# A two-layer linear-attention and Mish kernel: another order of work in its first block

## The chip, the cores and the metric

The kernel runs on one core of a Trainium2 chip. The metric is the device time of one execution in microseconds (us). The median of the three runs of the kernel before is 1381.55 us (1381.36 to 1382.13).

## What is computed

Two equal layers act on x of 2048 rows by 640 columns, in fp32. Each layer adds a linear attention of the normalized rows, and then a dense block of the normalized rows:

```python
q, k, v = split(layernorm(x) @ wqkv)              # 32 heads of 20
pq, pk  = q @ w_phi[h], k @ w_phi[h]              # per head, 20 x 20
phi     = concat(softmax(p), softmax(-p))         # 40 features for a head, of pq and of pk
kv, z   = phi_k^T v, sum of phi_k over the rows
x = x + ((phi_q kv) / (phi_q z + 1e-6)) @ wo
x = x + mish(layernorm(x) @ w1 + b1) @ w2         # 640 -> 1536 -> 640
```

Both layers use the same weights.

## The kernel before

**Tiling.** The rows are worked in 8 blocks of 256, each block as two tiles of 128 rows. Columns go in 5 chunks of 128 (KD = 5) where they are contracted. Every operand of a large product is split into a high part in the fp32r format (an ACT copy) and a low part that is the rest (a subtraction), and a product is three matmuls: high by high, high by low, low by high. One projection of one row tile (`project`, L329, its matmuls L344) is thus 2 column halves by 5 chunks by 3 = 30 matmuls of 128 x 320.

**Stages of a layer.** `attend_first` (L387) goes over the blocks. For each row tile it makes keys k, values v and queries q. `features` (L355) turns a k or q projection into softmax features, with ACT, VectorE (DVE) and GpSimd (POOL: the subtraction L369 of queries, the multiplication L379). Keys and values are summed over all rows into one PSUM tile `kva` (L416), and the query features are written to DRAM. `attend_second` (L549) reads them back, applies kv and the output weights wo, and prepares the weights of the dense block; `dense` (L677) does the rest. In the second layer the folded query and key weights come back from DRAM, where the first layer put them (`spill_qk_weights`, L187).

**Folding.** The matrix w_phi of a head is multiplied into the query and key columns of wqkv once, in the first layer. The host lays w_phi out as `phi_bd`, 120 x 6 x 120: block-diagonal groups of 6 heads (120 rows), and a sixth group of 2 heads (40 rows). `load_raw` (L212) fetches the transposed weights (`wqk_t`) in five tiles of 120 rows and one of 40; `fold_phi` (L227) multiplies chunk by chunk. For each of the 5 chunks there are two halves: columns 0 to 360 (tiles 0 to 2) and 360 to 640 (tiles 3 to 5), each with three matmul calls (L237), then the ACT copy L242 and the VectorE subtraction L243 that split the result. A call of plain fp32 is two matmul instructions in the trace, so a fold is 60 instructions.

**The first block of the first layer** (L446 to L460) is the place of the change. SP issues the DMAs. `tc.manual_schedule(engines={SP})` makes SP's issues keep the order written: half of phi, three raw tiles of the query weights, x of block 0, the other half of phi, the other raw tiles. `fetch_normed(0)` (L389) takes the row statistics (`norm_stats`, L246, on VectorE; `norm_scale`, L255, on POOL and VectorE). `normed(0, xt).all()` scales the two row tiles on ACT and turns them: `Transposed.step` (L271) turns 2 chunks of both row tiles on TensorE (four transposes by the identity, L280; two in the last step), and splits the result (ACT L285 through `act`, VectorE L286). Then come the query fold, values' weights (`load_v_weights`, L167, each chunk through `split`, L123, into a staging tile), and the raw key weights.

**The loop over blocks** (L465) follows. In block 0 the order is v0, q0, v1, k0, q1, k1, with the key fold ahead of k0 (L480). While block b is worked, x of block b + 1 is fetched and its statistics taken (at n = 0), scaled (n = 2) and turned (n > 2). Behind block 1, `load_o_weights` (L205) runs `make_five` (L193) to its end: five fetches of wo, five ACT copies (L148) and five POOL subtractions (L149).

**What sets the order of instructions.** The whole stands in a block that the framework schedules by a simulated timeline (L812): each engine's instructions go out in the order that the scheduler finds, except on engines named in a `manual_schedule`, which keep the order written. `act` (L110) chains ACT's instructions that go through it; `tc.issue_after(ins)` puts an engine's following instructions behind `ins`. A tile of a pool takes a buffer that is free: 4 row tiles (tag xn), 2 v tiles, 5 big tiles, and in PSUM 4 tiles of one bank (`one_tile`) and 2 of two banks (`mm_tile`).

Of the kernel before, what the change touches and what calls it, by code (L numbers as in the profile page):

```python
# [16 lines left out]
P = 128  # L17
# [24 lines left out]
def kernel(  # L42
# [42 lines left out]
    make_identity(nc, ident)  # L85
    b1s = const.tile([P, KF], F32, name="b1s")
# [21 lines left out]
    last_act = [None]  # L108

    def act(*args, **kw):  # L110

        if last_act[0] is None:
            ins = nc.scalar.activation(*args, **kw)
        else:
            with tc.issue_after(last_act[0]):
                ins = nc.scalar.activation(*args, **kw)
# [6 lines left out]
    def split(hi, lo, src, stage):  # L123

        st = stage()[:, :D]
        nc.sync.dma_start(st, src)
# [39 lines left out]

    def load_v_weights():  # L167

        ws = [r1_pair(k) for k in range(KD)]
        for k in range(KD):  # L170
            split(ws[k][0][:, D:2 * D], ws[k][1][:, D:2 * D], wv[k * P:(k + 1) * P, :],
                  (row_tile, row_tile, v_tile, v_tile, big_tile)[k])
# [32 lines left out]
    def load_o_weights():  # L205
        return list(make_five(KD, lambda k: wo[k * P:(k + 1) * P, :]))[1:]

# [4 lines left out]
    def load_raw(which, ts=range(6)):  # L212

        raw = []
        for t in ts:
            rows = 120 if t < 5 else 40
# [6 lines left out]
            nc.sync.dma_start(r[:n], wqk_t[which * D + t * 120:which * D + t * 120 + n, :])  # L223
# [3 lines left out]
    def fold_phi(ws, bd, raw):  # L227

        pss = {}
        for k, c in ((0, 0), (1, 0), (2, 0), (3, 0), (0, 1), (1, 1), (2, 1), (3, 1), (4, 0), (4, 1)):  # L230
# [3 lines left out]
            ps = pss[k][c]  # L234
            for t in range(3 * c, 3 * c + 3):
                r, rows = raw[t]
                nc.tensor.matmul(ps[:, (t % 3) * 120:(t % 3) * 120 + rows],  # L237
                                 r[:rows, k * P:(k + 1) * P], bd[:rows, t, :rows],
                                 start=True, stop=True)
# [147 lines left out]
    def attend_first(layer, x_src, first):  # L387


        def fetch_normed(b):  # L390
            if layer:
                return load_turned(n2_d[b], [row_tile] * 3)
            xt = fetch(x_src, b)
# [38 lines left out]
        def values(xts, i, v):  # L432
            vv = v.rearrange("p (h d) -> p h d", d=DH + 1)
            act(vv[:, :, DH], ident[:, :H], AF.Copy, scale=0.0, bias=1.0)
            if i < BT:
                pv = project(xts, i, kv_ws, D, [one_tile(), one_tile()])
# [9 lines left out]
        if first is None:  # L446
            with tc.manual_schedule(engines={mybir.EngineType.SP}):
                bd = big_tile()[:120, :720].rearrange("p (t c) -> p t c", t=6)
                nc.sync.dma_start(bd[:, :3], phi_bd[:, :3])
# [445 lines left out]
```

## Time and profile before

| | |
|---|---|
| Median of the runs | 1381.55 us |
| Profiled execution, its own time | 1381.04 us |
| Its span, first to last instruction | 1379.0 us |
| Mean granted TensorE clock | 0.999 |
| TensorE (PE) busy | 1364.3 us, 99% of the span |
| VectorE (DVE) busy | 1077.0 us, 78% |
| ScalarE (ACT) busy | 583.3 us, 42% |
| GpSimd (POOL) busy | 441.0 us, 32% |

How to read the profile: times count from the span's start. A row of the timeline has the start, the length, the engine, the line of the kernel, the operation, out<-in by the program's names, the shapes, and how many instructions are merged in it; in brackets stands the idle time before it and what ended it. Matmuls overlap in the pipeline and their ends are modelled, so the distance between starts says more than a length. PEld is the loading of stationary operands. A row of the window view has the stretch, its length, each engine's busy time with its instructions, TensorE's granted clock, the DMA engines' share and GB/s. A row of DMA issues has out<-in, the issuing queue, the count, KB of one and the median us from issue to landing.

### The profile page before, as it was taken

How to read it: one execution, taken by the hardware profiler on the slowest of the kernel's cores; microseconds unless marked ns; L12 is line 12 of the kernel's file. 1: busy time of each engine (PE TensorE's matmuls, PEld its weight loads, DVE VectorE, ACT ScalarE, POOL GpSimd, SP SyncE). 2: the span in 40 equal slices, each digit the busy share in tenths (PEclk: the TensorE clock that was granted, in tenths of full speed). 3: DMA queues.
4: the chain of work that ended last, by engine and by line, in shares of the span. 5: the costliest groups of instructions: out<-in, count | busy, mean ns of one | idle time of the engine just before them, and what ended most of it. 6: DMA issues, size and time to landing. Idle time of an engine off the chain costs nothing.

```text
span 1379.0 us, 30804 instructions
## 1 busy us (share of the span) xinstructions
PE 1364.3 (99%) x12866; PEld 1350.7 (98%) x12866; DVE 1077.0 (78%) x1820; ACT 583.3 (42%) x971; POOL 441.0 (32%) x334
## 2 busy tenths in 40 slices
PE   7999999999999999999999999999999999999998
PEld 7999999999999999999999999999999999999998
DVE  5799977886698887788769898988668776677775
ACT  4444434222355444545454333432235444354443
POOL 1353543353322221222234434453342111111112
PEclk9999999999999999999999999999999999999999
DMA  8532433779624533344473433458965321333200
GB/s 321 173 67 62 73 54 61 211 227 316 227 68 96 115 90 62 80 116 96 117 262 74 95 59 59 70 117 274 297 239 163 77 53 45 97 96 96 77 20 19
DMA packets 350277, 169.67 MB, mean 123 GB/s; under 512 B 287098, under 2 KB 323690, under 8 KB 350138
## 3 DMA queue, kind: packets, MB, share of 16 engines
q1 hardware_dynamic: 350137, 167.72, 45.0%
q8 instruction: 100, 1.64, 0.5%
q14 instruction: 40, 0.32, 0.1%
HBM read 104.76 MB, written 62.91 MB: 122 GB/s over the span
## 4 chain that ended last, share of the span: by engine, by line
PE 94%; DVE 2%; DMA 1%; issue 1%; POOL 0%; SPq 0%; ACT 0%; DVEq 0%; POOLq 0%; ACTq 0%
PE mm L344 26%; PE one L691 24%; PE mm L733 24%; PE one L344 12%; PE mm L569 3%; PE one L280 2%; PE one L416 2%; PE mm L237 1%; DMA raw<-in_wqk_t 1%; DVE m L368 1%; PE one L237 0%; DMA v<-in_wv 0%; DVE big L371 0%; DVE r L377 0%; DMA raw<-in_wo 0%
## 5 line engine op out<-in xcount | busy, mean ns | idle before, releaser
L733 PE MATMUL mm<-r2h,ol 128*128 128x320 f32 x1280 | 305.0, 309 | 0.3 <-ACT ol L716 0.3
L717 POOL TENSOR_TENSOR ol<-big,ol 128x512 fp32r<-128x512 f32 (+1 forms) x98 | 130.4, 1330 | 483.6 <-ACT ol L716 407.4
L691 PE MATMUL one<-xtl,r1h 128*128 128x256 f32 x960 | 268.2, 279 | 0.0
L691 PE MATMUL one<-xth,r1l 128*128 128x256 f32 x960 | 268.0, 279 | 0.0
L691 PE MATMUL one<-xth,r1h 128*128 128x256 f32 x960 | 265.9, 279 | 0.0
L733 PEld LDWEIGHTS mm<-r2h,ol 128*128 128x128 f32 x1280 | 219.2, 188 | 0.6 <-ACT ol L716 0.6
L733 PE MATMUL mm<-r2l,ol 128*128 128x320 f32 x640 | 197.3, 309 | 0.0
L344 PE MATMUL mm<-r1h,xth 128*128 128x320 f32 x600 | 187.5, 312 | 0.0
L344 PE MATMUL mm<-r1h,xtl 128*128 128x320 f32 x600 | 185.8, 310 | 0.4 <-DVE xtl L286 0.4
L344 PE MATMUL mm<-r1l,xth 128*128 128x320 f32 x600 | 186.0, 310 | 0.0
L691 PEld LDWEIGHTS one<-xtl,r1h 128*128 128x128 f32 x960 | 180.4, 188 | 0.0
L691 PEld LDWEIGHTS one<-xth,r1l 128*128 128x128 f32 x960 | 180.4, 188 | 0.0
L691 PEld LDWEIGHTS one<-xth,r1h 128*128 128x128 f32 x960 | 179.6, 188 | 0.0
L706 DVE TENSOR_SCALAR big<-big 128x512 f32<-128x512 f32 (+1 forms) x98 | 56.4, 575 | 110.6 <-ACT big L704 110.4
L379 POOL TENSOR_TENSOR r<-r,r 128x1280 f32<-128x1280 f32 x32 | 76.6, 2395 | 154.3 <-DVE r L378 148.5
L733 PEld LDWEIGHTS mm<-r2l,ol 128*128 128x128 f32 x640 | 120.2, 188 | 0.0
L708 ACT ACTIVATE big<-big,two 128x512 f32<-128x512 f32 (+1 forms) x98 | 70.3, 717 | 116.0 <-DVE big L707 116.0
L704 ACT ACTIVATE big<-one,b1s 128x256 f32<-128x256 f32 x192 | 81.0, 468 | 90.1 <-PE one L691 89.6
L716 ACT ACTIVATE ol<-big 128x512 fp32r<-128x512 f32 (+1 forms) x98 | 61.0, 623 | 136.3 <-DVE big L715 136.2
L344 PEld LDWEIGHTS mm<-r1h,xth 128*128 128x128 f32 x600 | 112.7, 188 | 0.8
L344 PEld LDWEIGHTS mm<-r1h,xtl 128*128 128x128 f32 x600 | 112.7, 188 | 0.7 <-DVE xtl L286 0.6
L344 PEld LDWEIGHTS mm<-r1l,xth 128*128 128x128 f32 x600 | 112.8, 188 | 0.1
(128 smaller groups left out, 3124.0 us busy)
## 6 DMA issues: line engine op xcount, KB each, us to landing
e_d<-r SPq DMA_DIRECT2D x128, 160.0 KB, 4.0
big<-e_d SPq DMA_DIRECT2D x32, 640.0 KB, 7.3
x_d<-xt SPq DMA_DIRECT2D x23, 640.0 KB, 3.6
xt<-x_d SPq DMA_DIRECT2D x22, 640.0 KB, 4.4
n_d<-xn SPq DMA_DIRECT2D x176, 80.0 KB, 2.3
xt<-in_x SPq DMA_DIRECT2D x16, 640.0 KB, 6.8
xn<-x_d SPq DMA_DIRECT2D x28, 320.0 KB, 4.4
v<-n_d SPq DMA_DIRECT2D x30, 256.0 KB, 3.1
```

Source lines behind the costliest of these rows:

```text
L280: nc.tensor.transpose(ps[:, c, t * P:(t + 1) * P], self.rows[t][:, (c0 + c) * P:(c0 + c + 1) * P], ident)
L344: nc.tensor.matmul(ps[:, :HC], a[:, sl], r, start=(k == 0 and n == 0), stop=(k == KD - 1 and n == 2))
L379: nc.gpsimd.tensor_tensor(eg, eg, r.unsqueeze(2).to_broadcast([P, 2 * H, DH]), op=ALU.mult)
L416: nc.tensor.matmul(kva[32 * j:32 * j + DH + 1, 40 * r:40 * r + 40], v[:, (DH + 1) * h:(DH + 1) * (h + 1)], e[:, 40 * h:40 * h + 40], start ...
L569: nc.tensor.matmul(po[64 * q:64 * q + 64, c, GW * j:GW * j + w], phs[g][:n, s0:s0 + 64], kvb[:n, g, :w], start=True, stop=True)
L691: nc.tensor.matmul(ph[:, j, :], l, r, start=(n == 0), stop=(n == 3 * KD - 1))
L704: exps[0] = nc.scalar.activation(part(ta, 0)[:, j - js.start], ph[:, j, :], AF.Exp, bias=b1s[:, 2 * pr + j:2 * pr + j + 1]).ins
L706: nc.vector.tensor_scalar_min(e, e, E_CAP)
L708: nc.scalar.activation(r, n, AF.Ln, bias=two)
L716: nc.scalar.activation(ah[:, js], n, AF.Copy)
L717: nc.gpsimd.tensor_tensor(al[:, js], n, ah[:, js].bitcast(F32), op=ALU.subtract)
L733: nc.tensor.matmul(pys[t][:, c, :HC], l[:, j, sl], r, start=(f == 0 and n == 0), stop=(f == KF - 1 and n == 2))
```

## The change

1. **A constant is turned first.** Behind `make_identity`, 58 transposes of the identity go into one PSUM tile that nobody reads.
2. **Another order, by hand, on five engines.** `written()` is a `manual_schedule` of PE, SP, ACT, DVE and POOL. In it stand: x of block 0 and its statistics; the five chunks of values' weights; phi; the raw query and key weights; x of block 1 (kept as `early`). Then the first chunk of values' weights is split, x is scaled (row tile 0 on ACT, row tile 1 on VectorE), and the splits of the other chunks alternate with the three steps of turning. v0 follows, chunk by chunk for both halves, and then the query fold. In the loop v0 is left out of block 0.
3. **Folding in chunks of 6, 4 and 4 heads in the second half.** The second half takes 120, 80 and 80 rows in place of 120, 120 and 40. A corner of `bd` is zeroed by VectorE and filled by two small DMAs.
4. **Late output weights.** Behind block 1 only three rows of wo are fetched; one of the five chunks is split at the start of each of the blocks 2 to 6, behind the last instruction of `act`. This holds for both layers. The fourth and fifth fetch go out at blocks 2 and 3, the fifth into a row tile.
5. Block 2's x is fetched and its statistics taken behind the last subtraction of the key fold (`folded[0]`).

The diff, cut to its core:

```diff
+    warm = one_tile()
+    for _ in range(58):
+        nc.tensor.transpose(warm[:, :P], ident, ident)
...
+        with tc.manual_schedule(engines={getattr(mybir.EngineType, e) for e in (
+                "PE", "SP", "Activation", "DVE", "Pool")}):
+            yield
...
-        if last_act[0] is None:
+        if last_act[0] is None or in_written[0]:
             ins = nc.scalar.activation(*args, **kw)
...
-    def split(hi, lo, src, stage):
-
-        st = stage()[:, :D]
-        nc.sync.dma_start(st, src)
+    def split(hi, lo, st):
...
+    def fetch_v(k):
+
+        st = (row_tile, row_tile, v_tile, v_tile, big_tile)[k]()[:, :D]
+        nc.sync.dma_start(st, wv[k * P:(k + 1) * P, :])
+        return st
...
-            rows = 120 if t < 5 else 40
+            rows = 120 if t < 4 else 80
...
-            nc.sync.dma_start(r[:n], wqk_t[which * D + t * 120:which * D + t * 120 + n, :])
+            c0 = which * D + (t * 120 if t < 5 else D - rows)
+            nc.sync.dma_start(r[:n], wqk_t[c0:c0 + n, :])
...
-                nc.tensor.matmul(ps[:, (t % 3) * 120:(t % 3) * 120 + rows],
-                                 r[:rows, k * P:(k + 1) * P], bd[:rows, t, :rows],
+                nc.tensor.matmul(ps[:, n:n + rows], r[:rows, k * P:(k + 1) * P], bd[:rows, t, :rows],
                                  start=True, stop=True)
+                n += rows
...
-            nc.vector.tensor_tensor(lo, ps[:, :n1 - n0], hi.bitcast(F32), op=ALU.subtract)
+            folded[0] = nc.vector.tensor_tensor(lo, ps[:, :n1 - n0], hi.bitcast(F32), op=ALU.subtract).ins
...
-            xt = fetch(x_src, b)
+            xt = fetch(x_src, b) if b > 1 else early
...
-            with tc.manual_schedule(engines={mybir.EngineType.SP}):
+            with written():
+                xt = fetch(x_src, 0)
+                mvs = [norm_stats(t, xt) for t in range(BT)]
+                kv_ws = [r1_pair(k) for k in range(KD)]
+                raws = [fetch_v(k) for k in range(KD)]
                 bd = big_tile()[:120, :720].rearrange("p (t c) -> p t c", t=6)
-                nc.sync.dma_start(bd[:, :3], phi_bd[:, :3])
-                raw = load_raw(0, range(3))
-                xt = fetch_normed(0)
-                nc.sync.dma_start(bd[:, 3:], phi_bd[:, 3:])
-                raw += load_raw(0, range(3, 6))
-                nxt = normed(0, xt).all()
+
+                nc.vector.memset(bd[:80, 5, :80], 0.0)
+                nc.sync.dma_start(bd[:40, 5, :40], phi_bd[80:120, 4, 80:120])
+                nc.sync.dma_start(bd[40:80, 5, 40:80], phi_bd[:40, 5, :40])
+                nc.sync.dma_start(bd[:, :5], phi_bd[:, :5])
+                raw_q = load_raw(0)
+                raw = load_raw(1)
+                early = fetch(x_src, 1)
+
+                def make_v(k):
+                    split(kv_ws[k][0][:, D:2 * D], kv_ws[k][1][:, D:2 * D], raws[k])
+
+                make_v(0)
+                norm_scale(0, mvs)
+                xn = [row_tile() for _ in range(BT)]
+                act(xn[0], xt[:, 0, :], AF.Identity, bias=stats[:, 0, 1, 0:1], scale=stats[:, 0, 0, 0:1])
+                nc.vector.tensor_scalar(xn[1], xt[:, 1, :], stats[:, 0, 0, 1:2], stats[:, 0, 1, 1:2],
+                                        op0=ALU.mult, op1=ALU.add)
+                nxt = Transposed(xn)
+                for k in range(1, KD):
+                    make_v(k)
+                    if k < 4:
+                        nxt.step()
+                vs0 = [v_tile() for _ in range(BT)]
+                pv = [one_tile(), one_tile()]
+                for k in range(KD):
+                    for c in range(2):
+                        project_half(pv[c], nxt, 0, kv_ws, D, c, range(k, k + 1))
+                next(values(nxt, 0, vs0[0], pv))
                 q_ws = [r2_pair(k) for k in range(KD)]
-                fold_phi(q_ws, bd, raw)
-                kv_ws = load_v_weights()
-                raw = load_raw(1)
+                fold_phi(q_ws, bd, raw_q)
...
+            if 2 <= b < 2 + KD:
+                with tc.issue_after(last_act[0]):
+                    o_ws.append(next(o_gen))
...
-                        xt = fetch_normed(b + 1)
+                        with tc.issue_after(folded[0]) if b == 1 and not layer else nullcontext():
+                            xt = fetch_normed(b + 1)
...
+                if begun and n == 0:
+                    continue
...
-                o_ws = load_o_weights()
+                o_gen = make_five(KD, lambda k: wo[k * P:(k + 1) * P, :])
+                next(o_gen)
+                o_ws = []
```

More of the change, by code (lines that the diff above doesn't have):

```diff
@@ L475, in attend_first @@
                 order = ("k0", "k1", "v0", "v1", "q0")
-            vs = [v_tile() for _ in range(BT)]
+            begun = b == 0 and not layer
+            vs = vs0 if begun else [v_tile() for _ in range(BT)]
+            if 2 <= b < 2 + KD:
+                with tc.issue_after(last_act[0]):
+                    o_ws.append(next(o_gen))
             for n, (kind, t) in enumerate(order):
```

19 lines of the change are left out of this document (11 added, 8 removed).

## The prediction

> **What bounds the kernel now.** I read the page first, then TensorE's waits, then its timeline over the first 50 us, then the other engines over the same stretch. The first rows give the span, TensorE's share (PE), and two entries of its waits (total us, times, longest).
>
> ```profile
> span 1379.0 us, 30804 instructions
> PE 1364.3 (99%) x12866; PEld 1350.7 (98%) x12866; DVE 1077.0 (78%) x1820; ACT 583.3 (42%) x971; POOL 441.0 (32%) x334
> ...
> PE mm L237 <- DMA raw<-in_wqk_t: 7.9, 3, 4.4
> ...
> PE mm L344 <- DVE xtl L286: 0.4, 1, 0.4
> ```
>
> TensorE is idle for 14.7 us of 1379.0, and 7.9 of these are three waits for the raw query and key weights (in_wqk_t) at the very start. So the kernel is a line of TensorE work laid end to end; a change gains what it takes out of the start, or out of TensorE's own instructions. The timeline (start, length, instructions; consecutive matmuls overlap, so I use distances between starts) shows the start:
>
> ```profile
> 4.42 1.18 PE L237 MATMUL mm<-big,raw 120*128 120x120 f32 x4 [4.42 <-DMA raw<-in_wqk_t]
> 6.41 2.08 PE L237 MATMUL mm<-big,raw 120*128 120x120 f32 x8 [0.81 <-DMA raw<-in_wqk_t]
> 11.19 2.21 PE L237 MATMUL mm<-big,raw 120*128 120x120 f32 x8 [2.70 <-DMA raw<-in_wqk_t]
> 13.32 1.07 PE L237 MATMUL mm<-big,r 40*128 40x40 f32 x4
> 14.33 0.90 PE L280 MATMUL one<-ident,xn 128*128 128x128 f32 x3
> 15.02 1.47 PE L237 MATMUL one<-big,raw 120*128 120x120 f32 x6
> 16.29 1.70 PE L280 MATMUL one<-ident,xn 128*128 128x128 f32 x7
> 17.78 1.06 PE L237 MATMUL mm<-big,raw 120*128 120x120 f32 x6
> ...
> 35.70 0.82 PE L237 MATMUL mm<-big,raw 120*128 120x120 f32 x6
> 36.36 0.83 PE L237 MATMUL one<-big,raw 120*128 120x120 f32 x6
> ...
> 39.25 0.70 PE L237 MATMUL one<-big,raw 120*128 120x120 f32 x4
> 39.89 0.41 PE L237 MATMUL one<-big,r 40*128 40x40 f32 x2
> 40.23 0.70 PE L237 MATMUL mm<-big,raw 120*128 120x120 f32 x4
> ...
> 42.18 1.31 PE L280 MATMUL one<-ident,xn 128*128 128x128 f32 x10
> 43.33 0.83 PE L237 MATMUL mm<-big,raw 120*128 120x120 f32 x6
> ```
>
> Two things beside the waits. TensorE is slow at first: the seven turns (transposes) at 16.29 take 17.78 - 16.29 = 1.49 us, 0.213 each; the ten at 42.18 take 1.15, 0.115 each. The speed doubles near 18 us, which the granted clock of the window view does not show (it reads 1.00 throughout). And a fold half with 40-row matmuls is dear: six 120-row ones take 36.36 - 35.70 = 0.66 us (0.11 each), but the half of four 120-row and two 40-row ones takes 40.23 - 39.25 = 0.98.
>
> At 35.70, where the key fold begins, TensorE has done 60 fold instructions of the query fold, 10 turns, and 90 projection matmuls (L344: v0, q0, v1). I take this as the **mark**. A projection matmul costs 0.1466 us, from 28 in 4.10 us in the chain of waits:
>
> ```profile
> 31.75 4.10 PE one L344 x28
> ```
>
> **The change, part by part.** In the new order TensorE does: 58 turns of the constant, 10 turns of x, v0 (30 matmuls), query fold (60), then q0 and v1 (60) to the mark. Call V the end of v0. Behind V, at full speed and without waits, the mark is at V + 60 x 0.11 (6.67 with the half's 0.667) + 60 x 0.1466 (8.80) = V + 15.47.
>
> *When x is ready to turn.* The rows: the first DMAs, their sizes, and the old path from x to its turns.
>
> ```profile
> 0.72 0.46 SPq L449 DMA_DIRECT2D big<-in_phi_bd  x1
> raw<-in_wqk_t SPq DMA_DIRECT2D x10, 320.0 KB, 6.3
> big<-in_phi_bd SPq DMA_DIRECT2D x2, 168.8 KB, 7.3
> xt<-in_x SPq DMA_DIRECT2D x16, 640.0 KB, 6.8
> 0.00:8.00 8.00, 2.76 (x11) 2.51 (x12) 0.09 (x2) 1.28 (x1) 0.69 (x6) 1.00 0.71 229
> 8.00:16.00 8.00, 5.30 (x23) 4.66 (x22) 4.79 (x16) 3.92 (x7) 1.09 (x3) 1.00 1.04 347
> 9.54 1.67 DVE L250 BATCH_NORM_STATS2 bn<-xt 128x6 f32<-128x320 f32 x4
> 12.89 0.92 ACT L113 ACTIVATE xn<-xt,stats 128x640 f32<-128x640 f32 x1 [3.90 <-DVE stats L262]
> 0.99 0.29 POOL masks.py:199 TENSOR_SCALAR_AFFINE_SELECT ident<-ident 128x128 f32<-128x128 f32 x1
> ```
>
> Phi and the first raw tile, 489 KB, had landed when TensorE began at 4.42. x is 640 KB and now first in the queue: 151 KB more at 229 to 347 GB/s is some 0.5 us, so x lands at about 4.9 (an estimate; the other end is the median landing of 6.8 us, 7.5). From the statistics to the first scaled row was 12.89 - 9.54 = 3.35 us, and the scaling takes 0.92; the second row now goes to VectorE beside it. x is ready at 4.9 + 4.3 = 9.2.
>
> *When the 58 turns end.* They need the identity, written at 1.28; say they start at 1.4. If the slow phase lasts c us, they end at 1.4 + c + (58 - c/0.213) x 0.115. The old trace bounds c: from 11.19 TensorE works without a pause until the speed-up near 18.3, 7.1 us; but up to 14.33 the starts lie 0.25 to 0.27 apart, and only from about 14.6 evenly 0.213, 3.6 us before it. So c is between 3.6 and 7.1, the turns end between 9.7 and 11.3; I take c = 5.3 and 10.5, the middle, since neither reading is nearer. They cover x's path, and cost what they overrun it by: 1.3 us. [...]
>
> *From the turns to V.* ACT and VectorE now alternate by hand between splits of values' weights and of turned x:
>
> ```profile
> 17.17 0.60 ACT L116 ACTIVATE xth<-one 128x512 fp32r<-128x512 f32 x1
> 19.02 0.68 DVE L286 TENSOR_TENSOR xtl<-one,xth 128x512 fp32r<-128x512 f32 x1
> 19.62 0.81 DVE L128 TENSOR_TENSOR r1l<-v,r1h 128x640 fp32r<-128x640 f32 x1
> 58.64 0.41 DVE L286 TENSOR_TENSOR xtl<-one,xth 128x256 fp32r<-128x256 f32 x1
> ```
>
> Four turns 0.45, xth 0.60, then VectorE in series: xtl 0.68, low 0.81, xtl 0.68, low 0.81, xtl 0.41, low 0.81 = 4.20; the last chunk's matmuls 0.9. Together 6.2 us; the 30 matmuls (4.4) hide beneath. So V = 10.5 + 6.2 = 16.7 (15.9 to 17.5 by c; 18.0 if x lands at 7.5).
>
> *Transfers.* The zeroing of a corner of bd stands behind the statistics on VectorE, and SP's phi and raw issues behind it, so these go out only from about 7; x and values' weights (2.29 MB) keep the queues busy until 9.3 at the window rates. The first three raw tiles end 3.56 MB, at 13.0, all six 4.42 MB, at 15.5. V is later, so the fold does not wait; the key rows have until 32.
>
> *The fold in 6, 4 and 4 heads.* Two calls of 80 rows replace one of 120 and one of 40; the count stays 60 (two instructions a call). I take 0.11 each, so 0.98 - 0.667 = 0.31 per second half, five of them in the key fold: 1.57 us. Bounds: nothing gained, or another 0.74 per fold if time goes with 80 columns instead of 120.
>
> The mark moves from 35.70 to 16.7 + 15.47 = 32.17, and everything behind it 1.57 further: 35.70 - 32.17 + 1.57 = **5.1 us**. (In short: the change is worth 21.8 - V.)
>
> *Late output weights.* The five ACT copies and five POOL subtractions, with their DMAs, go from block 1 to blocks 2 to 6, in both layers, and one row buffer is held from block 3 to 6 (three remain, two are needed).
>
> ```profile
> 53.07 3.11 POOL L149 TENSOR_TENSOR r2l<-raw,r2h 128x640 fp32r<-128x640 f32 x2 [7.42 <-ACT r2h L148]
> 54.94 1.92 DVE L371 TENSOR_TENSOR big<-m,big 128x640 f32<-128x640 f32 x1
> 62.66 0.82 DVE L371 TENSOR_TENSOR r<-m,r 128x640 f32<-128x640 f32 x1
> 76.00:92.00 16.00, 15.58 (x224) 14.98 (x223) 16.00 (x24) 6.55 (x11) 8.78 (x8) 1.00 0.34 67
> 92.00:120.00 28.00, 28.00 (x253) 27.72 (x252) 26.84 (x34) 11.04 (x16) 13.57 (x9) 1.00 0.38 72
> 180.00:210.00 30.00, 30.00 (x358) 29.52 (x358) 22.94 (x28) 12.39 (x18) 12.00 (x6) 1.00 0.29 45
> 840.00:870.00 30.00, 30.00 (x324) 29.75 (x323) 26.98 (x29) 10.68 (x16) 14.34 (x7) 1.00 0.40 77
> ```
>
> A VectorE subtraction beside POOL's takes 1.92 instead of 0.82. VectorE is full from 76 to 92 (16.00 of 16) and TensorE waits 0.4 us for xtl there; taking POOL's work out gives about that back. In the later blocks VectorE has slack of 1.2 us in 28 (at 92) to 7 in 30 (at 180), in the second layer 3 in 30 (at 840), and a subtraction a block costs it 1.1. I count zero, between a gain of 0.4 and the loss below. Block 2's statistics now stand behind the key fold's last subtraction on VectorE; its rows are turned a block later, so nothing waits for that. All else behind the mark moves with TensorE, since VectorE's features start when a projection ends.
>
> The profiled execution took 1381.04 us, 2.0 around its span; it becomes 1375.9. The median of the runs shown is 1381.55; the same 5.1 off it gives 1376.4.
>
> **The rivals.**
>
> *The constant turns do not release the clock* (it ends on the other side). If turning doesn't count as work for whatever doubles the speed, 58 turns at 0.213 end at 13.8; four slow turns and xth bring 15.25; then projection matmuls at twice 0.1466 until c = 5.3 us have passed (18 of them, to 20.6), the other 12 at full speed: V = 22.3, a loss of 0.5 us, 1382.1. It loses as soon as V is over 21.8, that is with c over 4; at c = 7.1 V is 23.2 and the time 1383.0. For it: the granted clock, which would tell, reads 1.00 even where the turns are slow, so the trace cannot rule it out. Against it: the even stretch before the speed-up, from 14.6, holds nine turns beside eight fold instructions, while the twelve fold instructions from 11.19 released nothing. [...]
>
> *The late output weights make VectorE the bound.* A POOL subtraction of 1.56 us (half of 3.11) delays VectorE in full, and TensorE with it. In blocks 2 to 4 of the first layer that is 4.7 us back, up to 1381.1; in the five of the second layer, too, another 7.8, up to 1388.9. The change loses once 5.1 of these 12.5 us reach TensorE. For it: 26.84 of 28 busy at 92. Against: the slack above, which holds 1.1 a block almost everywhere, and a subtraction need not meet one of VectorE's.
>
> *The change doesn't do what it says*, because the raw rows come late and the fold waits in place of v0. At 229 GB/s to the end the first three would be there at 15.5 and all six at 19.3. The fold needs the first three at V = 16.7 and the others after four first halves, at 16.7 + 4 x 0.667 = 19.4. So even then it just does not wait; each us later costs one. I give it 2 us at most (1378.4), inside the forecast's range.
>
> **How the numbers follow.** Forecast 0.66, its own range 1373.8 (c = 3.6, 0.8; cheaper 80-row calls, 1.5; the 0.4 wait) to 1378.5 (x at 7.5, or late rows). VectorE bound in the first layer alone 0.11, between 1376.4 and 1381.1; about half of it less than 2.8 us under the old median. In both layers 0.05, 1384 to 1389. Slow turns 0.15, 1381 to 1383. Slow turns and a bound VectorE 0.03: 1382.1 + 4.7 = 1386.8. A measurement of this kernel tells about 0.2%, 2.8 us, from no change. Faster: 0.66 + 0.06 = 0.72; same: 0.05 + 0.15 = 0.20; slower: 0.05 + 0.03 = 0.08. The first two cases hold 0.77; up to 1381.5 the range takes in a fifth of the slow turns, 0.03, and holds 0.80: 1373.8 to 1381.5.
>
> **What would show it.** In the changed profile: the waits for in_wqk_t (7.9) gone; the 58 turns at 0.213 first and 0.115 later, ending near 10.5; v0 ending near 16.7; the query fold straight after it, each half 0.67 with no long second half; the key fold's first matmul near 32; the xtl wait near 86 not over 0.5 us. Wrong if the turns stay at 0.213 to the end, if the fold waits on DMA, or if TensorE's waits for VectorE in blocks 2 to 6 of either layer add up to over 1 us.

## The result: slower by 0.3%

The changed kernel takes 1386.65 us (median of 7 runs, 1385.36 to 1387.3), the kernel before 1381.83 beside it (7 runs, 1381.36 to 1382.47). The ratio is 1.0029, interval [1.002, 1.0039]: the change costs 4.8 us where 5.1 were forecast as a gain. The profiled execution took 1385.58 us. Its page shows hardly a trace of it: 99% for TensorE, as before.

```profile
span 1383.8 us, 30926 instructions
PE 1367.3 (99%) x12924; PEld 1353.5 (98%) x12924; DVE 1077.7 (78%) x1822; ACT 581.5 (42%) x970; POOL 442.0 (32%) x334
```

TensorE's waits over the whole span answer to the rows of before. The 7.9 us for in_wqk_t are gone. In their place stand waits for VectorE's xtl, ACT's r, POOL's big and VectorE's r1l:

```profile
PE mm L360 <- DVE xtl L302: 3.6, 4, 1.4
PE mm L360 <- ACT r L129: 1.5, 1, 1.5
...
PE one L432 <- POOL big L395: 1.0, 1, 1.0
PE mm L251 <- DVE r1l L257: 1.0, 1, 1.0
```

(Lines moved: the projection's matmul L344 is L360 now, the fold's L237 is L251, the turns L280 are L296, the kva matmul L416 is L432, L89 is the constant's turn.)

The start came out as forecast, or 0.7 us better. In TensorE's timeline the 58 turns and the ten of x are followed by v0 (from 11.00) and, at 15.96, by the query fold, without a wait for a DMA:

```profile
1.34 8.43 PE L89 MATMUL one<-ident 128*128 128x128 f32 x58 [1.34 <-POOL ident masks.py:199]
9.66 1.31 PE L296 MATMUL one<-ident,xn 128*128 128x128 f32 x10
...
15.96 0.82 PE L251 MATMUL mm<-big,raw 120*128 120x120 f32 x6
...
18.63 0.58 PE L251 MATMUL mm<-big,raw 120*128 120x120 f32 x4
...
19.27 0.61 PE L251 MATMUL one<-big,raw 120*128 120x120 f32 x4
...
31.03 0.82 PE L251 MATMUL one<-big,raw 120*128 120x120 f32 x6
...
35.40 0.67 PE L251 MATMUL one<-big,raw 120*128 120x120 f32 x4 [0.41 <-ACT v L129]
...
37.26 0.67 PE L251 MATMUL mm<-big,raw 120*128 120x120 f32 x4 [0.97 <-DVE r1l L257]
```

The key fold starts at 31.03 instead of 35.70, a second half takes 19.27 - 18.63 = 0.64 us instead of 0.98. (The query fold's last chunk came later, at 22.93 and 27.71, between projection matmuls.) So TensorE had won what it should. Where it lost it again shows when the n-th projection matmul of one trace is set beside the n-th of the other. I call the difference the **lead** (us that the kernel is ahead of before). All leads of this text, by the time in before:

```
                                         50     104    134    840    910    950
after                                  +4.0    +0.4   +0.4   +0.3   -3.4   -4.5
e1 late weights undone                 +3.3    -0.3   -0.3   -3.1   -3.1   -2.7
e2 before + late weights               -0.2    +0.1   +0.1   -0.4   -3.8   -6.1
e3 before + fold in 6, 4, 4            +1.0    +1.0   +1.0   -0.6   -0.6   -0.5
e4 no constant turns                   +0.4    -3.3   -3.3   -5.1   -8.2   -9.8
e5 statistics of block 2 put back      +2.4    +2.6   +2.6   +2.0   -2.1   -3.2
e6 late weights at n == 3              +3.0    -0.6   -0.6   -1.5   -1.8   -2.3
e7 e5 and e6 together                   0.0    +0.4   +0.4   -0.2   -0.2   -0.8
e8 parts 1 to 3 alone                  -2.3    -5.5   -5.5   -6.6   -6.6   -6.2
e9 e7, key fold ahead of q0            +3.1    +1.8   +1.8   +1.7   +1.6   +1.1
e11 e8, key fold ahead of q0           +3.4    +2.3   +2.3   +1.6   +1.6   +1.5
```

Each row is one profiled execution, set beside the one of before (1381.04 us), which is among before's faster ones. Executions of one kernel differ by some us, so the end of a row need not agree with the medians. In some of them the granted clock was at half for steps of 3.41 us, which cost 1.7 us each (an estimate: half of a step; in e10 below a fall made 86 turns 1.67 us longer) and are in the leads: one at 39.5 us in e4 (whose execution, 1392.54 us, was the slowest of its five), two in e1, at 71.7 and 710.0, and those of e7 and e8 that are shown below.

The first row has the whole story: about 1 us is missing at 50 (4.0 instead of 5.1), 3.6 go between 50 and 104, and 4.8 between 840 and 950, in blocks of the second layer. The window view shows the same stretches idle: of 45 us TensorE worked 41.70, and of 30 us each 29.58, 28.62 and 29.04, where in before all three were full (before had 44.58 of the 45, the last row).

```profile
60.00:105.00 45.00, 41.70 (x515) 39.95 (x514) 41.42 (x51) 18.82 (x26) 23.14 (x13) 1.00 0.43 90
840.00:870.00 30.00, 29.58 (x319) 29.06 (x318) 26.17 (x28) 11.27 (x16) 14.62 (x8) 1.00 0.37 68
870.00:900.00 30.00, 28.62 (x313) 28.11 (x312) 26.76 (x28) 11.39 (x16) 14.91 (x8) 1.00 0.40 72
900.00:930.00 30.00, 29.04 (x314) 28.40 (x314) 27.34 (x30) 9.97 (x14) 14.48 (x7) 1.00 0.51 112
...
60.00:105.00 45.00, 44.58 (x539) 43.47 (x538) 45.00 (x54) 21.19 (x29) 25.58 (x15) 1.00 0.41 83
```

### The profile page after: what moved, and what is told of

Its sections match the earlier page's. It is cut to its first block, busy times and chain, and to the rows that moved or that the text cites. A ratio compares the mean times of both kernels' runs of the same rounds, so it can differ in the third digit from the quotient of the medians.

```text
span 1383.8 us, 30926 instructions
## 1 busy us (share of the span) xinstructions
PE 1367.3 (99%) x12924; PEld 1353.5 (98%) x12924; DVE 1077.7 (78%) x1822; ACT 581.5 (42%) x970; POOL 442.0 (32%) x334
## 5 line engine op out<-in xcount | busy, mean ns | idle before, releaser
L360 PE MATMUL mm<-r1h,xth 128*128 128x320 f32 x600 | 187.7, 313 | 2.4 <-ACT r L129 1.5
L360 PE MATMUL mm<-r1h,xtl 128*128 128x320 f32 x600 | 186.0, 310 | 3.6 <-DVE xtl L302 3.6
L360 PE MATMUL mm<-r1l,xth 128*128 128x320 f32 x600 | 185.9, 310 | 0.0
L395 POOL TENSOR_TENSOR r<-r,r 128x1280 f32<-128x1280 f32 x32 | 77.9, 2435 | 149.1 <-DVE r L394 143.6
L360 PEld LDWEIGHTS mm<-r1h,xtl 128*128 128x128 f32 x600 | 112.7, 188 | 4.8 <-DVE xtl L302 4.6
L360 PEld LDWEIGHTS mm<-r1h,xth 128*128 128x128 f32 x600 | 112.7, 188 | 3.8 <-ACT r L129 1.6
L360 PEld LDWEIGHTS mm<-r1l,xth 128*128 128x128 f32 x600 | 112.8, 188 | 0.3 <-issue 0.3
```

The lines of the kernel that those rows point to most:

```text
L360: nc.tensor.matmul(ps[:, :HC], a[:, sl], r, start=(k == 0 and n == 0), stop=(k == KD - 1 and n == 2))
L395: nc.gpsimd.tensor_tensor(eg, eg, r.unsqueeze(2).to_broadcast([P, 2 * H, DH]), op=ALU.mult)
```

## The experiments

The theories. For the second layer: the late subtraction of an output weight stands in POOL's queue ahead of the queries' subtraction, VectorE waits for that, and the delay adds up from block to block (theory A); its rivals are a row buffer held too long (G) and contention that any extra POOL work brings. For 50 to 104 us: block 2's statistics, put behind the key fold, turn the order of VectorE's and POOL's work round (E); the rival is that VectorE, full there, takes back any head start whatever its order (C). For the key fold: TensorE arrives before VectorE is done with the splits. Seven kernels were run for these, and four more after a surprise in the seventh. Each was run beside the kernel before on the same chip.

**The late output weights, undone (e1) and alone (e2).** e1 is the changed kernel with the weights split in block 1 again; e2 is the kernel before with the late weights as its only change.

```diff
-            if 2 <= b < 2 + KD:
-                with tc.issue_after(last_act[0]):
-                    o_ws.append(next(o_gen))
...
-                o_gen = make_five(KD, lambda k: wo[k * P:(k + 1) * P, :])
-                next(o_gen)
-                o_ws = []
+                o_ws = list(make_five(KD, lambda k: wo[k * P:(k + 1) * P, :]))[1:]
```

> The changed kernel with part 4 undone alone: all five chunks of the output weights are split behind block 1 again, in both layers. Theory A (in the second layer the POOL subtraction of the output weights, 1.56 us, stands ahead of the queries' subtraction on POOL, VectorE waits for that one, and the lag adds up over blocks 2 to 6): the 4.9 us that TensorE loses between 838 and 935 us come back, the second layer runs as before, and the time is 1381 to 1382. Theory B (the second layer's loss comes from elsewhere in the new order, for instance from where the first layer leaves the schedule): the loss stays, 1385 to 1387.

> The kernel before with part 4 alone: the output weights split chunk by chunk at the start of blocks 2 to 6, in both layers. Theory A: the second layer loses 4 to 5.5 us on its own, with nothing of the first block changed: 1386 to 1388. Theory B: no loss, 1381 to 1382.5.

e1: 1381.98 us, ratio 1.000 [0.999, 1.001]. e2: 1386.5 us, ratio 1.0024 [1.0014, 1.0033]. In e1 the lead stands still from 840 to 910 (the 2.8 it loses from 134 to 840 hold the half-clock step at 710.0), in e2 it falls by 5.7 from 840 to 950, by the same waits as in the changed kernel. e2's rows of TensorE's waits from 820 to 945 us:

```profile
PE mm L344 <- DVE xtl L286: 2.5, 3, 1.4
PE one L416 <- POOL big L379: 1.3, 1, 1.3
```

So part 4 costs some 5 us, all of it in the second layer; in the first e2 loses nothing (+0.1 at 134). How, the changed kernel's POOL shows early in that layer: the split of an output weight (L159), then the queries' subtraction (L385).

```profile
793.23 1.56 POOL L159 TENSOR_TENSOR r2l<-raw,r2h 128x640 fp32r<-128x640 f32 x1 [1.90 <-ACT r2h L158]
794.76 1.85 POOL L385 TENSOR_TENSOR r<-r,m 128x640 f32<-128x640 f32 x1
```

VectorE's next step waits for that subtraction:

```profile
796.64 0.83 DVE L387 TENSOR_TENSOR r<-m,r 128x640 f32<-128x640 f32 x1 [1.17 <-POOL r L385]
```

From 780 to 930 us these waits of VectorE add up to 4.7 us in the changed kernel; in before they were one wait of 1.3.

```profile
DVE r L387 <- POOL r L385: 4.7, 4, 1.2
```

That the delay adds up shows in e2, where nothing of the first block is changed. VectorE's first step on the queries of four blocks (L371) starts at 794.23, 823.77, 852.86 and 882.51 us, in before at 793.87, 822.02, 849.59 and 877.76: 0.4, 1.8, 3.3 and 4.8 us later. In the first layer the same lag comes and goes (0.4 us at 147, 2.8 at 179, -0.1 at 214), so VectorE catches up there.

**The fold alone (e3), and no constant turns (e4).** e3 is the kernel before with the second half in 120, 80 and 80 rows; e4 is the changed kernel without the 58 turns. They change the head start from both sides, so that theory C can be read.

```diff
-            rows = 120 if t < 5 else 40
+            rows = 120 if t < 4 else 80
...
```

```diff
-    warm = one_tile()
-    for _ in range(58):
-        nc.tensor.transpose(warm[:, :P], ident, ident)
```

> The kernel before with the second fold half in chunks of 120, 80 and 80 rows alone. It takes some 3 us of TensorE's instructions out of the first 50 us. Theory C (VectorE is the bound from about 60 to 105 us, so any head start of TensorE in the first block is gone when VectorE has caught up): TensorE is 1.5 to 3 us earlier at 60 us and less than 0.7 us earlier at 120 us; the time is 1381.2 to 1382. Theory D (a head start moves everything behind it, as the prediction had it): 1378.5 to 1379.5.

> The changed kernel without the 58 turns of the constant. TensorE then starts slow: v0 ends 2 to 5 us later than 15.96. Theory C: that delay, too, is taken up before 120 us, so the time stays within 0.8 us of the changed kernel's 1386.65. Theory D: the time is 2 to 5 us longer, 1388.5 to 1391.5.

e3: 1381.0 us, ratio 0.9987 [0.9977, 0.9996], the one kernel of this study whose interval lies below 1. It keeps its lead of 1.0 from 50 to 134, through the stretch where VectorE is full; by 840 the lead of its profiled execution is gone (-0.6), in part by a wait of 1.2 us for VectorE's xt, so the 0.13% rests on the medians alone. e4: 1388.1 us, ratio 1.0044 [1.0028, 1.0061]. Its v0 ended at 17.93 instead of 15.96, so the turns are worth 2.0 us there. It loses 3.7 us between 50 and 104 with hardly any lead to lose. Both speak against C: the loss doesn't depend on the head start. The times settle nothing: both lie between the forecasts of C and D. e3's lead is smaller than its 1.6 to 3 us of fold, since it waits 8.5 us at the start where before waited 7.9, and so is 0.6 behind at 20 us:

```profile
PE mm L239 <- DMA raw<-in_wqk_t: 5.5, 2, 4.3
PE mm L239 <- DVE mv L254: 3.0, 1, 3.0
```

**Block 2's statistics put back (e5), the late weights' step behind the head of the queue (e6).** e5 undoes part 5. e6 leaves everything but moves the step of part 4 from the start of the block to n == 3.

```diff
-                        with tc.issue_after(folded[0]) if b == 1 and not layer else nullcontext():
-                            xt = fetch_normed(b + 1)
+                        xt = fetch_normed(b + 1)
```

```diff
-            if 2 <= b < 2 + KD:
-                with tc.issue_after(last_act[0]):
-                    o_ws.append(next(o_gen))
...
+                if n == 3 and 2 <= b < 2 + KD:
+                    with tc.issue_after(last_act[0]):
+                        o_ws.append(next(o_gen))
```

> The changed kernel with part 5 undone alone: block 2's x and statistics no longer have to stand behind the key fold's last subtraction. In the changed kernel and in the run without turns TensorE loses 3.6 us against the kernel before between 60 and 105 us, whether it comes there 4.0 us early or 0.4. Theory E (an order of work does it: behind the edge the statistics of two blocks, 3.9 us, stand on VectorE at 44 to 48, ahead of k0's features, POOL takes the second query's subtraction ahead of the first query's multiplication, and the first queries' store ends 8.6 us after ACT needs its buffer): without the edge that loss is 1 us or less, the second layer still loses its 5, and the time is 1383 to 1384.5. Theory F (VectorE's load does it, whatever the order): no change, 1386 to 1387.

> The changed kernel with the step of the output weights put at the fourth projection of blocks 2 to 6 (n = 3) in place of the block's start, where the queries' subtractions on POOL are over; the row tile is held from block 3 to 6 as before. Theory A (the place on POOL, ahead of the queries' subtraction): the loss of 5 us in the second layer goes to under 1, 1381 to 1382.5. Rival G (the row tile that is held leaves three, and the second layer's fetch of the turned rows takes three for each block; or any POOL work in these blocks costs that much): the loss stays, 1385 to 1387.

e5: 1385.45 us, ratio 1.0026 [1.0015, 1.0037]; nothing is lost from 50 to 104 (+2.4 to +2.6), and the second layer loses its 5 us as before. e6: 1383.32 us, ratio 1.001 [0.9999, 1.0022]; the second layer loses 0.8 instead of 4.8, with the same five subtractions and the same row buffer held, and the first loses 3.7 still. So by the leads A and E hold, each in its place, and G falls. The times show less. e5 is 1.2 us faster than the changed kernel by the medians (by the ratios 0.3), not 3.6, and above E's 1383 to 1384.5: it had 1.6 us less lead at 50, after a wait of 1.66 us for r1l at 41.61 in its key fold. e6 lies above A's 1381 to 1382.5. e6 also moves ACT's copy that goes with the subtraction; that the place on POOL counts rests on the rows above.

E's chain can be read row by row. In the changed kernel the statistics of two blocks stand at 44.28 and 46.10, ahead of block 1's first feature (L384):

```profile
44.28 1.66 DVE L266 BATCH_NORM_STATS2 bn<-xt 128x6 f32<-128x320 f32 x4
...
46.10 1.66 DVE L266 BATCH_NORM_STATS2 bn<-xt 128x6 f32<-128x320 f32 x4
47.68 1.53 DVE L384 TENSOR_REDUCE m<-big 128x32 f32<-128x640 f32 x2
```

They take VectorE's time ahead of those features. On POOL the order of two instructions is turned round, too: a query tile's subtraction (L385) goes ahead of the multiplication (L395) that the tile before it needs.

```profile
53.27 1.28 POOL L385 TENSOR_TENSOR r<-r,m 128x640 f32<-128x640 f32 x1
54.54 2.92 POOL L395 TENSOR_TENSOR r<-r,r 128x1280 f32<-128x1280 f32 x1
```

In e5 the multiplication goes first, as in before:

```profile
54.00 2.37 POOL L395 TENSOR_TENSOR r<-r,r 128x1280 f32<-128x1280 f32 x1 [10.66 <-DVE r L394]
56.33 1.28 POOL L385 TENSOR_TENSOR r<-r,m 128x640 f32<-128x640 f32 x1
```

and VectorE's transposition of those features begins at 56.41,

```profile
56.41 1.51 DVE L440 STREAM_TRANSPOSE r<-r 128x1280 f32<-128x1280 f32 x1 [0.82 <-POOL r L395]
```

while in the changed kernel it begins at 61.79:

```profile
57.47 0.81 DVE L387 TENSOR_TENSOR r<-m,r 128x640 f32<-128x640 f32 x1
...
61.79 1.50 DVE L440 STREAM_TRANSPOSE r<-r 128x1280 f32<-128x1280 f32 x1
```

POOL's order is the smaller part of these 5.4 us: the multiplication ends at 57.46 there and at 56.37 in e5, 1.1 us apart. For the other 4.3 us VectorE, without a pause from 57.47 to 61.79, does other features' work that now stands ahead.

The store to DRAM follows it, ACT waits for the store's buffer, and TensorE for ACT (the 1.5 us of L360 for r in the list of waits, at 70.47):

```profile
69.71 0.70 ACT L129 ACTIVATE r<-mm 128x640 f32<-128x640 f32 x1 [8.63 <-DMA e_d<-r]
```

**Both together (e7): a miss.** With both losses mended the forecast gain should have appeared.

> Both edits: no edge to the fold, and the output weights at n = 3. Theories A and E: the head start of about 4 us is carried through both layers, 1377.5 to 1379.5, below both kernels. Theory F with A: 1381 to 1382.5. Rival G: 1383 to 1387.

e7: 1382.19 us, ratio 0.9995 [0.9984, 1.0006], the time that theory F with A had, but not for its reason. Both losses are gone (+0.4 to -0.2 from 104 to 910), but there was no lead to keep: 5.6 us at 27 us, none at 50. In the folds TensorE waited for splits and for a PSUM tile, and then its granted clock fell to half for 6.83 us, which cost some 3.4. The two rows are the stretch before the fall and the fall:

```profile
35.24:38.65 3.41, 2.13 (x17) 1.75 (x17) 2.79 (x6) 3.41 (x10) 1.27 (x1) 1.00 0.37 120
38.65:45.48 6.83, 6.50 (x30) 6.11 (x30) 4.69 (x15) 1.49 (x4) 1.07 (x3) 0.50 1.02 397
```

**Parts 1 to 3 alone (e8), and the key fold moved ahead of q0 (e9, e11).** e8 is e1 and e5 together. e9 is e7, and e11 is e8, with another order in block 0, so that the splits of the fold don't meet the features of q0 on VectorE:

```diff
-                order = ("v0", "q0", "v1", "k0", "q1", "k1")
+                order = ("v0", "v1", "q0", "k0", "q1", "k1")
...
-                if b == 0 and n == (1 if layer else 3):
+                if b == 0 and n == (1 if layer else 2):
```

> Parts 1 to 3 of the change alone: the output weights are split in block 1 again and block 2's statistics stand where they stood. Theory (the loss comes from the order in which part 4's subtractions and block 2's statistics stand in POOL's and VectorE's queues): no loss of TensorE's lead between 60 and 105 us and none between 846 and 935 us; the lead is what the key fold's waits leave of 5 us, 2.4 at 51 us in the kernel that has the late output weights and this place of the statistics; so 1379 to 1381 (ratio 0.998 to 0.9995), and 1.7 to 3.4 us more in executions whose granted clock drops to half for a while. Rival (VectorE and POOL in block 1 of the first layer take any lead, since the eager output weights stand there): the lead falls to 0 by 105 us and the time is 1382 to 1383 (ratio 1.000 to 1.001).

> The changed kernel with the output weights' step behind the heads' queue (n == 3), block 2's statistics where they stood, and in the first block of layer 1 v0, v1, then the key fold, then q0, k0, q1, k1: the key fold's splits on VectorE then don't meet the features of q0. Theory (the key fold waits on VectorE because q0's features stand between its splits): no wait of TensorE for r1l or r2l in the key fold, hence no pauses close together and no drop of the granted clock behind it; the lead at 51 us is 4 or more and is held to the end: 1377.5 to 1379.5 (ratio 0.996 to 0.998). Rival (features that begin 4 us later leave VectorE behind, and TensorE waits for xtl or the features in block 1 in place of the key fold): lead down to 0 to 1 by 105 us, 1381 to 1383 (ratio 0.999 to 1.001).

> Parts 1 to 3 of the change alone, as in the kernel that gave 1386.56 us with a mean granted clock of 0.994 to 0.999 in its runs, and the order v0, v1, key fold, q0, k0, q1, k1 in the first block. Theory (that kernel's loss of 0.3% comes from pauses in the key fold, and a granted clock at half behind them): without the features of q0 between the key fold's splits the pauses stay under some 1.3 us in 3.4, the clock is 0.998 to 1.000 in the runs, and the time is 1380 to 1383 (ratio 0.998 to 1.001). Rival (the 0.3% is lost in block 1, where the eager output weights stand ahead of the features, and the clock is only a companion): 1385 to 1387, with the loss between 50 and 105 us in the records.

e8 was a miss for both theories: 1386.56 us, ratio 1.0031 [1.0022, 1.004]. It loses nothing in the second layer, and still it is as slow as the full change. Its rows show why: two waits, for ACT's v in the key fold and for ACT's r at 92 us, and two falls of the clock, behind stretches in which TensorE worked 1.92 and 1.43 of 3.42 us (two rows of the timeline, then four of the window view).

```profile
38.79 1.11 PE L296 MATMUL one<-ident,xn 128*128 128x128 f32 x4 [1.46 <-ACT v L129]
...
92.38 0.42 PE L360 MATMUL mm<-r1h,xth 128*128 128x320 f32 x1 [1.99 <-ACT r L129]
...
35.13:38.55 3.42, 1.92 (x15) 1.59 (x14) 1.55 (x2) 3.42 (x7) 1.26 (x1) 1.00 0.02 10
38.55:48.79 10.24, 9.78 (x40) 9.19 (x41) 6.72 (x18) 3.27 (x9) 2.59 (x5) 0.50 0.85 321
89.74:93.16 3.42, 1.43 (x10) 1.16 (x9) 3.42 (x4) 1.54 (x2) 2.52 (x1) 1.00 0.37 64
93.16:96.57 3.41, 3.41 (x59) 3.08 (x60) 3.41 (x7) 1.31 (x4) 2.72 (x3) 0.50 0.01 2
```

The 13.65 us at a clock of 0.50 cost 6.8 us (an estimate, half of them). The lead of 5.7 at 27 us, less 3.0 of waits in the folds, 2.0 at 92 us and these 6.8, leaves -6.1; the table has -6.6 at 840. It was no single execution: the mean granted clock of e8's 11 runs was 0.994 to 0.999, of e11's 0.998 to 1.000. e11: 1381.76 us, ratio 0.9998 [0.9989, 1.0007]; its profile has no fall ahead of its last 0.5 us, and of 3.0 us of pauses in e8's folds (0.99 in the last half of the query fold, the rest in the key fold) 1.7 are left:

```profile
PE mm L251 <- DVE r1l L257: 1.1, 2, 0.6
PE mm L360 <- DVE r1l L257: 0.6, 1, 0.6
```

So the order alone is worth 4.8 us against e8, by the medians. The mean granted clock over the 11 runs is 0.9960 in e8 and 0.9994 in e11; the difference makes 4.7 us of 1386, so the half-clock steps fit nearly all of it. e8's rival, that the eager weights in block 1 take any lead, doesn't hold as it stands: e11 has them too and keeps 2.3 us at 104. But e8 lost 3.2 us between 50 and 104, where its theory had none, and what the eager weights do to its wait there wasn't separated. e9: 1382.8 us, ratio 0.9999 [0.999, 1.0008], also without a fall in its profile ahead of the last 0.7 us; its forecast of 1377.5 to 1379.5 was a miss, and the rival was nearer, since only 1.8 us of lead outlived block 1 and none shows in the median.

**Pauses by themselves (e10).** Is it the pauses that bring the clock down? A prelude ahead of the changed kernel has turns and nothing else, and TensorE is made to wait for 1 to 12 small copies on VectorE, 38 times. It ran once.

```diff
-    for _ in range(58):
-        nc.tensor.transpose(warm[:, :P], ident, ident)
...
+        for k, reps in [(k, 1) for _ in range(3) for k in (1, 2, 3, 4, 5, 6, 7, 8, 10, 12)] + [(1, 3)] * 4 + [(2, 2)] * 4:
+            for _ in range(reps):
+                for i in range(k):
+                    nc.vector.tensor_copy(warm[:, P:2 * P], warm[:, :P])
+                for _ in range(4):
+                    nc.tensor.transpose(warm[:, :P], ident, ident)
+            for _ in range(86):
+                nc.tensor.transpose(warm[:, :P], ident, ident)
```

> The changed kernel with a prelude ahead of everything else: in place of the 58 constant turns 90 of them, and then 38 times a pause of TensorE (it waits for 1 to 12 copies on VectorE; in the last eight cases three short pauses or two, with four turns between) and 86 to 98 turns behind it. Only the prelude is read: the pauses' lengths and the granted clock behind each. Theory (the clock is set in steps of 3.41 us, and a step in which TensorE is idle for more than some 1.3 to 1.5 us halves the clock of the next): behind pauses under 1.2 us no drop, behind pauses over 3 us always one, between them it goes by where the pause lies in its step; every drop lasts 3.41 us or a multiple and costs half of that; short pauses add up within a step. Rival (a drop needs a whole step idle, so only pauses of 3.4 us and more bring one, and the drops in the other kernels have another cause, such as the many cores' power or the transfers): no drop behind any pause under 3.4 us. The time is longer by the prelude, some 400 to 500 us, and tells nothing.

The clock fell 11 times in the prelude, each time a whole number of 3.41 us behind its first release at 5.69, for 3.41 or 6.83 us. The windows are cut on these steps, and each step is shown with the one behind it; the granted clock is the third number from the end:

```profile
193.43:196.84 3.41, 1.59 (x15) 1.35 (x13) 1.61 (x6) 0.00 (x0) 0.00 (x0) 1.00 0.00 0
196.84:200.25 3.41, 3.17 (x29) 3.17 (x30) 0.19 (x1) 0.00 (x0) 0.00 (x0) 1.00 0.00 0
323.13:326.55 3.42, 1.36 (x13) 1.12 (x12) 1.80 (x6) 0.00 (x0) 0.00 (x0) 1.00 0.00 0
326.55:329.96 3.41, 3.41 (x18) 3.41 (x17) 0.00 (x0) 0.00 (x0) 0.00 (x0) 0.50 0.00 0
...
121.75:125.16 3.41, 1.28 (x12) 1.03 (x10) 1.89 (x7) 0.00 (x0) 0.00 (x0) 1.00 0.00 0
125.16:128.57 3.41, 1.49 (x7) 1.49 (x8) 1.70 (x6) 0.00 (x0) 0.00 (x0) 0.50 0.00 0
128.57:131.99 3.42, 3.42 (x18) 3.42 (x17) 0.00 (x0) 0.00 (x0) 0.00 (x0) 0.50 0.00 0
```

The pauses at 195.02 and 324.25 are equally long, 2.06 us. The first lies across the border of two steps, 1.82 us in the one and 0.24 in the other, and the clock stays; the second lies within one step and halves the next. One pause of 3.40 us, split into 1.92 and 1.48, did nothing:

```profile
112.98 0.66 PE L96 MATMUL one<-ident 128*128 128x128 f32 x4 [3.40 <-DVE one L94]
```

So the rival (a whole step idle) falls, and of the theory the limit: in these turns it lies between 1.92 and 2.06 us of idle time in a step, not at 1.3 to 1.5, and the pause of 3.40 us brought no fall. A step at half clock with 1.92 us idle (125.16) was followed by another at half, though as much in a step at full clock did nothing. What a fall costs, two rows show: 86 turns behind the pause at 195.02, which brought none, and 86 behind the next one, of 2.39 us within one step, 11.22 - 9.55 = 1.67 us more.

```profile
197.58 9.55 PE L98 MATMUL one<-ident 128*128 128x128 f32 x86
...
210.01 11.22 PE L98 MATMUL one<-ident 128*128 128x128 f32 x86
```

The prelude doesn't tell whether short pauses add up, since its groups of them come to 1.5 us at most. e1 speaks for it: its step ahead of the fall at 71.7 held 2.21 us of idle time out of two waits, of 0.92 and 1.54 us.

In the folds and projections that limit is not the whole of it. In e7 and e8 falls came behind steps with 1.28 and 1.50 us idle (3.41 - 2.13, 3.42 - 1.92), while e5 had one with 1.58 and no fall. In e7 the first of the two steps at half had at most 0.33 us idle (6.83 - 6.50) and was still followed by another. Matmul ends are modelled there, and what else counts beside pauses stays open.

The changed kernel stands behind the prelude, and its key fold shows what the grid does: it has the same waits of 0.41 and 0.97 us as the profile without the prelude, but there a border at 35.95 (an estimate: nine steps of 3.41 behind the release at 5.23) divides them and the clock stays at 1.00, and here 1.08 us of idle time fall into one step (3.42 - 2.34) and the clock halves for 6.83 us:

```profile
517.69:521.11 3.42, 2.34 (x19) 2.00 (x18) 2.68 (x5) 3.42 (x10) 1.27 (x1) 1.00 0.30 81
```

## Why the prediction was wrong

*Right: the constant turns release the clock.* The window view, cut where the clock was released, has 18 matmuls in the 3.89 us up to 5.23 and 42 in the 4.43 us behind it, 0.22 and 0.105 us each:

```profile
1.34:5.23 3.89, 3.89 (x18) 3.89 (x19) 0.51 (x2) 0.65 (x1) 0.00 (x0) 1.00 0.85 288
5.23:9.66 4.43, 4.43 (x42) 4.30 (x41) 3.15 (x10) 1.73 (x3) 1.63 (x3) 1.00 0.97 314
```

c was 3.9 us (5.23 - 1.34), near the lower reading of 3.6 and below the 5.3 that I took; the turns ended at 9.7, not 10.5. No single c could have been right: with the same start of the turns it was 3.1 in e8 (release at 4.4) and 5.5 in e1 (6.9). These fp32 turns reached the faster rate by themselves: nothing but turns ran before 9.66, and in e10's prelude turns alone held it from 132 to 210 us (86 of them took 9.55 us, 0.11 each).

*Right: V, the fold, the transfers.* v0 ended at 15.96 (16.7 forecast), the fold's second half takes 0.64 to 0.67, no matmul of the folds waits on a DMA. The key fold began at 31.03, ahead of three of the 90 projection matmuls (0.44 us), so the mark stands at 31.47; the sum said 32.17. By this the gain at the key fold's end would be 5.1 + 0.7 us.

*Wrong, 1.4 us: "so the fold does not wait" was asked only of the transfers.* The key fold came 4.7 us earlier, but its splits on VectorE compete with q0's features, which begin when q0 ends, and in it are waits of 0.41 us (a PSUM tile that ACT's copy of v frees) and 0.97 (a split). With the rest that no wait shows, the lead at 50 us is 4.0.

*Wrong, 3.6 us: "Block 2's statistics now stand behind the key fold's last subtraction on VectorE; its rows are turned a block later, so nothing waits for that."* I looked at who waits for the statistics, and not at what they are put ahead of, nor that the scheduler sets the order of POOL's instructions anew when a time shifts. e5 gives the 3.6 back, by the lead.

*Wrong, 5 us: the late output weights, "I count zero".* This was the rival "make VectorE the bound": its price for the second layer was 7.8 at most, and the case that had it got 0.05. The measured time lies inside that case's 1384 to 1389 by luck: its sum had 4.7 us from the first layer, where the late weights cost nothing, and knew nothing of the statistics. The prediction's own sign of being wrong here came true: TensorE's waits for VectorE's xtl from 820 to 955 us add up to 2.6. The slack argument failed on two counts. The slack of 3 us in 30 was VectorE's mean over a block, while the delay is a queue's order: 1.56 us of POOL ahead of the one subtraction that VectorE's next step needs, once per block. And it adds up: VectorE doesn't catch up within a block of the second layer, so blocks 2 to 6 go on from one another's delay (0.4 to 4.8 us in e2) until TensorE waits for xtl. In the first layer, for which I feared it, it cost nothing (e2). The same five subtractions, three projections later in the block (e6), cost 0.8 in place of 4.8.

*"All else behind the mark moves with TensorE"* failed with these three: engines that were on time for a TensorE that started late were not for one that came 5 us earlier. The forecast 1376.4 and the 1386.65 differ by 10.2 us: 1.1 short at 50 us, 3.6, 4.8, and 0.4 in small steps elsewhere make 9.9; the rest is how the medians lie to the profiled executions. The changed kernel's three runs with a granted clock of 1.000, the profiled one among them, took 1385.36 to 1385.75 us, the four at 0.997 to 0.999 took 1386.65 to 1387.3; that fits a half-clock step or two behind the waits in the key fold, as in e10, but only the profiled run was traced.

The experiments left no version that beats both kernels by more than e3's 0.13%. Parts 1 to 3 with the better order (e11) kept 1.5 us of lead in its profile, and in the median none that the interval tells from 1; where these 1.5 go in the other runs wasn't settled, though clocks of 0.998 and 0.999 in five of its 11 runs fit another fall or two at 1.7 us each. Its six runs with a clock of 1.000 have a median of 1380.6, before's beside it with 1.000 one of 1382.0.

## What to carry to other kernels

When a stage is started earlier, list for every engine what its next instruction stands behind, since slack averaged over a block (here 3 us in 30) didn't hide a delay that sat ahead of one needed instruction and came again each block (1.56 us of POOL, 4.8 us late by the fourth block of e2). Before an instruction is moved "to where nobody waits for it", ask what it now goes ahead of, in each queue, in every stage that runs the same code. And a pause of TensorE can cost more than its length: where pauses filled 2.06 us of a 3.41 us clock step (e10's turns), or in the folds here sometimes 1.1 to 1.5 (e10, e7, e8), the next step ran at half speed.

## What the runs showed of the hardware

In e10's prelude each fall of the granted clock came a whole number of 3.41 us steps behind the first release at 5.69 us, and it lasted one step or two. The steps lie elsewhere in other executions: the first release came at 4.4 (e8) to 6.9 us (e1) where turns started at 1.3. In e10's turns a step with 2.06 us of idle time or more halved the clock of the next (11 of 11), and none with 1.92 or less at full clock did, so no whole step had to be idle, and of two pauses of 2.06 us one brought a step at half (324.25) and the other, across a border, none (195.02). In the folds falls came behind 1.08 (e10), 1.28 (e7) and 1.50 us (e8), too. In e10 a step at half made 86 turns 1.67 us longer (11.22 against 9.55); 1.7 us are 0.12% of this kernel, so by this estimate a run with one such step more is that much longer. The steps are not the whole spread: before's runs beside e5 to e7 lie from 1380.58 to 1385.41 us, and both of these had a granted clock of 1.000.
